# Attention and a three-way maxout layer: two steps' TensorE work issued together, the softmax normalised on ACT, output stages begun beside such a group

## The chip, the cores and the metric

The kernel runs on one core of one Trainium2 chip. The metric is the device time of one execution in microseconds. TensorE (PE, its weight loads PEld) multiplies matrices and transposes into PSUM, VectorE (DVE) and ScalarE (ACT) read PSUM and SBUF, GpSimd (POOL) works on SBUF only, and SyncE (SP) issues DMAs. POOL issues DMAs of its own too. Each engine works through its own queue in order, and semaphores hold an instruction until what it needs is there.

## The reference

There are two parts: a causal attention with a window of 128 positions and a distance bias per head, and on its output a layer that takes the maximum of three products and multiplies once more. Batch 8, 8 heads, 576 positions, 64 per head; 512 model columns, 768 hidden ones; all float32.

```python
scores = scale * np.matmul(q, k.transpose(0, 1, 3, 2))
bias = slopes[:, None, None] * (-np.abs(rel).astype(np.float32))[None, :, :]
mask = (rel >= 0) & (rel < window)
scores = np.where(mask, scores + bias[None], -1000000000.0)
scores = scores - np.max(scores, axis=-1, keepdims=True)
attn = np.exp(scores)
attn = attn / (np.sum(attn, axis=-1, keepdims=True) + 1e-09)
attn_out = np.matmul(attn, v)
# x: attn_out with the heads side by side, (8 * 576, 512)
h = np.maximum(np.maximum(x @ w1, x @ w2), x @ w3)
out = h @ w_out
```

## The kernel before, in words

**Attention.** A task t is one batch b and one pair of heads hp (32 tasks, four for each batch). A step (t, i) is a block of 128 query rows of a task, five for each task (the last has 64 rows), 160 steps in all. As the window is 128, a block of queries meets its own block of keys and the one before it. One step passes through four functions:

- `products` (L245) multiplies queries by keys on TensorE, 64 x 64 tiles side by side in the array, into the two banks of `scores`; one call covers two steps.
- `score` (L263): VectorE merges the two key blocks by a mask (L271 or L274), adds the bias and reduces to the row's extreme for each head (L286); ACT takes the exponential with a running sum into the tile p (L290, four buffers). After blocks 1, 3 and 4 it also adds 1e-9 to the sums (L296), takes the reciprocal (L299) and multiplies each p of the pair by it (L302), on POOL for even tasks of the first two batches and on VectorE otherwise.
- `turn` (L306): TensorE transposes p for both heads into the PSUM tile pt (L311, pool ps_t, one buffer); ACT copies it out (L315 for block 0, straight into pp; L318 into pr for the others); POOL cuts it into the two triangles of pp (L319, L323; four buffers).
- `mix` (L328) multiplies by v on TensorE (L345) into ps_x. After block 4 ACT copies the task's result to xk (L354).

**Dense layers.** Both products are done blockwise with seven block products in place of eight. A unit u is one such block product (L496): six matmuls of 288 columns for the expert stage (63 units for each batch), nine for the output stage (14 for each batch). ACT copies some units' results out of PSUM (L505), `put` (L436) combines the others on VectorE (L443 to L460), and `factors_h` (L404) splits the hidden blocks into a rounded part on ACT (L371) and a rest on POOL (L372), called hs, that the output stage multiplies. `factors_x` (L377) does the same for a batch's attention output, called xs. The units use the three PSUM banks ps_m. In batch 0 the weights are also unpacked and split (`convert`, `sums`, `part`; 120 calls through `weights`), and written to DRAM; later batches stream them back by a DMA that POOL issues once a buffer of a ring of two is free (`stream`, L218).

**Order.** There is no scheduler at run time: the list `events` (from L511) holds (due, call) pairs, the calls are made in order of due time, and each engine's queue is the order of those calls. Time is counted in steps, each batch's attention shifted by SHIFT = (0, 2, 5). Step s makes products at s if s is even, score at s, turn at s + 4.3, mix of blocks 0 and 1 of a task 7.4 steps after block 1, of blocks 2 to 4 7.4 steps after block 4. Batch b's expert units begin at `ready[b]`, just behind its last mix, and are spread evenly up to `ready[b + 1]`; batch b's 14 output units begin there, O_PACE = 0.36 steps apart, with `factors_x` of the next batch ahead of them. So while units of batch b run, the attention of batch b + 1 runs between them. `weights` is called once a step at s + 0.2, and twice a unit in batch 0. PSUM's eight banks are all in use: three ps_m, two scores, one pt, two ps_x.

Of the kernel before, what the change touches and what calls it, by code (L numbers as in the profile page):

```python
# [8 lines left out]
F32 = mybir.dt.float32  # L9
# [3 lines left out]
AF = mybir.ActivationFunctionType  # L13
ALU = mybir.AluOpType
# [1 line left out]

NEG = 1.0e30
LOAD_I = 1
LAG_T, LAG_X = 4, 7
GROUPS = (1, 4)  # L20
SHIFT = (0, 2, 5)
O_PACE = 0.36
RING = 2


# [4 lines left out]
def attention_maxout_kernel(  # L30
# [11 lines left out]
    nc = tc.nc  # L42
    P = 128
    B, NP, _, _, S = qk.shape
# [5 lines left out]
    NB = (S + P - 1) // P  # L50
    rows = [min(P, S - i * P) for i in range(NB)]
# [17 lines left out]
    ps_t = ctx.enter_context(tc.tile_pool(name="ps_t", bufs=1, space=PSUM))  # L69
# [16 lines left out]
        out=prev, in_=prev, pattern=[[1, P]], compare_op=ALU.is_gt, fill=0.0,  # L86
# [150 lines left out]
    pn, pp, xp, xk, stats = {}, {}, {}, {}, {}  # L237
# [25 lines left out]
    def score(t, i):  # L263
        b, hp = tasks[t]
        n = rows[i]
        ps, a = banks.pop((t, i))
        if i:
            mask = prev[:n].bitcast(mybir.dt.uint8)
            if a is None:
                for x in ps:  # L270
                    nc.vector.copy_predicated(x[:n, P:2 * P], mask, x[:n, :P])  # L271
            else:
                both = scores[:n, :, a * 2 * P:(a + 1) * 2 * P]
                nc.vector.copy_predicated(  # L274
                    both[:, :, P:], mask.unsqueeze(1).broadcast_to([n, 2, P]), both[:, :, :P],
                )
        p = s_p.tile([P, 2, P], F32, name="p", bufs=4)

        if i % 2 == 0:
            stats[t] = st_p.tile([P, 3, 2, 2], F32, name="st"), []  # L280
        st, two = stats[t]
        a = len(two)
        two.append(p)
        for j in range(2):
            s = s_p.tile([P, P], F32, name="s", bufs=3)
            nc.vector.tensor_tensor_reduce(  # L286
                out=s[:n], in0=ps[j][:n, P:2 * P], in1=(bias if i else bias0)[:n, 2 * hp + j, :],
                scale=-0.125, scalar=3.0e38, op0=ALU.add, op1=ALU.min, accum_out=st[:n, 0, a, j:j + 1],
            )
            nc.scalar.activation(  # L290
                p[:n, j], s[:n], AF.Exp, bias=st[:n, 0, a, j:j + 1], scale=-1.0, accum_out=st[:n, 1, a, j:j + 1]
            )
        pn[t, i] = p
        if i % 2 == 0 and i + 1 < NB:
            return
        nc.vector.tensor_scalar(  # L296
            out=st[:n, 1, :a + 1], in0=st[:n, 1, :a + 1], scalar1=1e-9, scalar2=None, op0=ALU.add
        )
        nc.vector.reciprocal(st[:n, 2, :a + 1], st[:n, 1, :a + 1])  # L299
        e = nc.gpsimd if t < 2 * NP and t % 2 == 0 else nc.vector  # L300
        for a, p in enumerate(two):
            e.tensor_tensor(  # L302
                out=p[:n], in0=p[:n], in1=st[:n, 2, a].unsqueeze(2).broadcast_to([n, 2, P]), op=ALU.mult
            )

    def turn(t, i):  # L306
        n = rows[i]
        p = pn.pop((t, i))
        pt = ps_t.tile([P, 2, P], F32, name="pt")
        for j in range(2):  # L310
            nc.tensor.transpose(out=pt[:, j, :n], in_=p[:n, j], identity=ident[:n, :n])  # L311
        w = pp_p.tile([P, 2, 2, P], F32, name="pp")
        pp[t, i] = w
        if i == 0:
            nc.scalar.copy(out=w[:, :, 0, :n], in_=pt[:, :, :n])  # L315
            return
        r = s_p.tile([P, 2, P], F32, name="pr", bufs=2)
        nc.scalar.copy(out=r[:, :, :n], in_=pt[:, :, :n])  # L318
        nc.gpsimd.affine_select(  # L319
            out=pp[t, i - 1][:, :, 1, :n], in_=r[:, :, :n], pattern=[[0, 2], [-1, n]],  # L320
            compare_op=ALU.is_gt, fill=0.0, base=0, channel_multiplier=1,
        )
        nc.gpsimd.affine_select(  # L323
            out=w[:n, :, 0, :n], in_=r[:n, :, :n], pattern=[[0, 2], [1, n]],
            compare_op=ALU.is_ge, fill=0.0, base=0, channel_multiplier=-1,
        )
# [187 lines left out]
    def at(when, what, *args):  # L514
        events.append((when, len(events), what, args))

    n_steps = NP * NB
    shift = [SHIFT[min(b, 2)] for b in range(B)]
    for t, (b, hp) in enumerate(tasks):
        for i in range(NB):  # L520
            s = t * NB + i + shift[b]
            if i == LOAD_I and t + 2 < len(tasks):
                at(s - 0.4, load, t + 2)
            if i == NB - 1 and t + 1 < len(tasks):
                at(s - 0.4, load_v, t + 1)
            if i == 0 and 0 < t < NP:
                at(s - 1, slopes, t)
            if (t * NB + i) % 2 == 0:
                at(s, products, t * NB + i)
            at(s, score, t, i)  # L530
            at(s + LAG_T + 0.3, turn, t, i)
            last = next(e for e in GROUPS if e >= i)
            at(s + last - i + LAG_X + 0.4, mix, t, i)

    ready = [n_steps * (b + 1) - 1 + LAG_X + 0.5 + shift[b] for b in range(B)]
    when = ready[0]
    for b in range(B):
        if b == 0:
            at(when, factors_x, 0, 0, 0)

        pace = (ready[b + 1] - when) / 63 if b + 1 < B else O_PACE
        for u in range(77 * b, 77 * b + 77):
# [3 lines left out]
            at(when, unit, u)  # L546
            when += pace if u < 77 * b + 63 else O_PACE
    for u in range(77 * B, 77 * B + 3):
# [49 lines left out]
```

## Time and profile before

| what | us |
|---|---|
| median of three runs | 872.14 |
| the runs | 865.38, 872.14, 874.06 |
| the profiled execution | 869.13 |
| its span, first to last instruction | 867.4 |
| granted TensorE clock, mean | 0.951 |

The profiled execution's own time lies 1.7 us above its span. The page gives each engine's busy time over the span; a busy TensorE may still be a slow one, as matmuls overlap and the modelled ends of the records are counted. In the table of stretches each engine has its busy time and, in brackets, its number of instructions; behind them stand the granted clock, the share of the DMA engines and GB/s. A group row names line, engine, operation, tiles and shape, then count, busy time and mean ns, then the idle time of the engine just ahead and who ended it. A wait row gives the total, the number of waits and the longest one.

### The profile page before, as it was taken

The numbers are of one execution on the slowest core, as the hardware profiler recorded it, in microseconds if no ns is written. First come the engines' busy times: TensorE is split into PE (matmuls) and PEld (weight loads), VectorE is DVE, ScalarE is ACT, GpSimd is POOL, SyncE is SP. The second block draws the span as 40 slices with busy tenths as digits, with TensorE's granted clock in tenths as the row PEclk, the third lists the DMA queues.
The fourth block names the chain that finished last, engine by engine and source line by source line (L and its number), as shares of the span: only waits on it lengthen the run. The fifth ranks groups of instructions, "written<-read, shape, count | busy, mean of one in ns | idle before, by whom it ended". The sixth has DMA issues, their size and how long they took to land.

```text
span 867.4 us, 17966 instructions
## 1 busy us (share of the span) xinstructions
PE 789.2 (91%) x6272; PEld 680.3 (78%) x6272; DVE 622.1 (72%) x1954; ACT 460.6 (53%) x1502; POOL 356.2 (41%) x580
## 2 busy tenths in 40 slices
PE   4779786777999999999999999999999999999897
PEld 2347565656988888887988798987889788989887
DVE  5789998899767866778577956777567957483452
ACT  6768666756555544555445544555456545442232
POOL 3543353213155423544255514544255525541332
PEclk7978897967999999999999999999999999999999
DMA  6653675662578638883577737883678537765761
GB/s 215 219 192 127 229 253 214 229 245 76 188 263 273 232 113 270 279 284 115 194 258 269 249 107 256 268 292 117 221 258 293 187 125 245 247 235 168 257 203 56
DMA packets 43402, 184.80 MB, mean 213 GB/s; under 512 B 4784, under 2 KB 13744, under 8 KB 34096
## 3 DMA queue, kind: packets, MB, share of 16 engines
q0 software_dynamic: 18144, 115.61, 39.9%
q1 hardware_dynamic: 25024, 67.97, 21.8%
q8 instruction: 50, 0.82, 0.4%
q14 instruction: 40, 0.33, 0.1%
q10 hardware_dynamic: 144, 0.07, 0.0%
HBM read 157.68 MB, written 25.95 MB: 212 GB/s over the span
## 4 chain that ended last, share of the span: by engine, by line
PE 60%; DVE 10%; issue 6%; ACT 6%; POOL 5%; DMA 3%; POOLq 0%; ACTq 0%; DVEq 0%; SPq 0%
PE ps_m L496 47%; PE ps_x L345 6%; PE ps_s L256 4%; POOL hs L372 3%; PE pt L311 3%; ACT p L290 2%; DMA wt<-keep 2%; DVE p L302 2%; DVE hq L458 1%; POOL pp L319 1%; DVE t L457 1%; ACT hs L371 1%; DVE t L375 1%; POOL pp L323 1%; DMA hs<-in_w_all 1%
## 5 line engine op out<-in xcount | busy, mean ns | idle before, releaser
L496 PE MATMUL ps_m<-xs,wt 128*128 128x288 f32 x3024 | 461.6, 306 | 22.3 <-DVE t L457 7.6
L496 PEld LDWEIGHTS ps_m<-xs,wt 128*128 128x128 f32 x3024 | 419.0, 192 | 53.8 <-DVE t L457 11.6
L290 ACT ACTIVATE p<-s,st 128x128 f32<-128x128 f32 (+1 forms) x320 | 126.0, 396 | 102.1 <-PE pt L311 78.2
L505 ACT COPY t<-ps_m 128x288 f32<-128x288 f32 x264 | 103.9, 398 | 138.3 <-PE ps_m L496 137.7
L496 PE MATMUL ps_m<-hs,ow 128*128 128x288 f32 x1008 | 156.3, 307 | 12.7 <-POOL hs L372 7.3
L496 PEld LDWEIGHTS ps_m<-hs,ow 128*128 128x128 f32 x1008 | 139.9, 193 | 25.9 <-POOL hs L372 11.4
L218 POOL DMA_DIRECT2D wt<-keep x126 | 69.8, 554 | 214.6 <-PE ps_m L496 170.5
L372 POOL TENSOR_TENSOR hs<-hq,hs 128x288 fp32r<-128x288 f32 x120 | 105.8, 890 | 51.6 <-ACT hs L371 51.3
L319 POOL TENSOR_SCALAR_AFFINE_SELECT pp<-pr 128x256 f32<-128x256 f32 (+1 forms) x128 | 63.3, 495 | 131.8 <-ACT pr L318 121.4
L345 PE MATMUL ps_x<-pp,v 128*64 128x256 f32 (+3 forms) x768 | 89.0, 338 | 15.7 <-POOL pp L319 13.1
L457 DVE TENSOR_TENSOR t<-ps_m,t 128x288 f32<-128x288 f32 x144 | 64.9, 451 | 43.2 <-PE ps_m L496 41.2
L286 DVE CUSTOM_DVE_ANT_0 s<-ps_s,bias 128x128 f32<-128x128 f32 (+1 forms) x300 | 77.7, 281 | 17.9 <-ACT p L290 12.7
L323 POOL TENSOR_SCALAR_AFFINE_SELECT pp<-pr 128x256 f32<-128x256 f32 (+1 forms) x128 | 65.2, 509 | 50.8 <-PE ps_x L345 50.8
L345 PEld LDWEIGHTS ps_x<-pp,v 128*64 128x64 f32 (+1 forms) x768 | 47.6, 140 | 42.9 <-POOL pp L319 18.0
L371 ACT CAST hs<-hq 128x288 fp32r<-128x288 f32 x120 | 50.2, 430 | 57.2 <-DVE hq L375 36.0
L256 PE MATMUL ps_s<-qk 64*64 64x192 f32 (+1 forms) x1080 | 69.6, 338 | 8.8 <-DVE st L286 4.7
L311 PE MATMUL pt<-ident,p 128*128 128x128 f32 (+1 forms) x320 | 64.1, 283 | 14.6 <-POOL p L302 7.7
L302 DVE TENSOR_TENSOR p<-p,st 128x256 f32<-128x256 f32 (+1 forms) x140 | 71.9, 545 | 1.8
L458 DVE TENSOR_TENSOR hq<-t,hq 128x288 f32<-128x288 f32 x144 | 70.0, 486 | 2.3
L274 DVE COPY_PREDICATED ps_s<-prev,ps_s 128x256 f32<-128x256 uint8 x120 | 50.4, 420 | 27.2 <-PE ps_s L256 26.3
L311 PEld LDWEIGHTS pt<-ident,p 128*128 128x128 f32 (+1 forms) x320 | 40.3, 145 | 30.9 <-POOL p L302 13.6
L290 ACT ACTIVATION_READ_ACCUMULATOR p<-s,st 128x1 f32 (+1 forms) x320 | 60.4, 189 | 0.0
(54 smaller groups left out, 714.0 us busy)
## 6 DMA issues: line engine op xcount, KB each, us to landing
wt<-keep POOLq DMA_DIRECT2D x63, 1024.0 KB, 7.0
wt<-keep POOLq DMA_DIRECT2D x63, 768.0 KB, 4.7
qk<-in_qk SPq DMA_DIRECT2D x31, 576.0 KB, 5.3
hs<-in_w_all SPq DMA_DIRECT2D x24, 512.0 KB, 5.9
v<-in_v SPq DMA_DIRECT2D x32, 320.0 KB, 4.7
keep<-wt SPq DMA_DIRECT2D x9, 1024.0 KB, 3.9
outT<-t SPq DMA_DIRECT2D x64, 144.0 KB, 1.8
keep<-wt SPq DMA_DIRECT2D x9, 768.0 KB, 5.1
```

Of the source, the lines that this page charges most:

```text
L256: nc.tensor.matmul(ps[j][d:d + D, o:o + k1 - k0], lhsT=qkt[t][j * D:(j + 1) * D, 0, q0:q0 + D], rhs=qkt[t][j * D:(j + 1) * D, 1, k0:k1], s ...
L286: nc.vector.tensor_tensor_reduce(out=s[:n], in0=ps[j][:n, P:2 * P], in1=(bias if i else bias0)[:n, 2 * hp + j, :], scale=-0.125, scalar=3. ...
L290: nc.scalar.activation(p[:n, j], s[:n], AF.Exp, bias=st[:n, 0, a, j:j + 1], scale=-1.0, accum_out=st[:n, 1, a, j:j + 1])
L302: e.tensor_tensor(out=p[:n], in0=p[:n], in1=st[:n, 2, a].unsqueeze(2).broadcast_to([n, 2, P]), op=ALU.mult)
L311: nc.tensor.transpose(out=pt[:, j, :n], in_=p[:n, j], identity=ident[:n, :n])
L323: nc.gpsimd.affine_select(out=w[:n, :, 0, :n], in_=r[:n, :, :n], pattern=[[0, 2], [1, n]], compare_op=ALU.is_ge, fill=0.0, base=0, channel ...
L345: nc.tensor.matmul(x[j * D:(j + 1) * D, c:c + e - a], lhsT=vv[:n, i, j * D:(j + 1) * D], rhs=w[:n, j].rearrange("p a b -> p (a b)")[:, a:e ...
L372: e.tensor_tensor(out=lo, in0=src, in1=hi.bitcast(F32), op=ALU.subtract)
L457: nc.vector.tensor_tensor(out=s, in0=ps, in1=e, op=ALU.add)
L458: nc.vector.tensor_tensor(out=h, in0=s, in1=h, op=ALU.max)
L496: nc.tensor.matmul(ps, lhsT=lt, rhs=rt, start=i == 0 and k in (0, 1, 4), stop=i == len(pairs) - 1, skip_group_check=True,)
L505: nc.scalar.copy(out=e, in_=ps)
```

## The change

Three constants change, `score` is cut in three, `turn` uses one pt tile for two steps, and the due times are rewritten. A step s with c = s rounded down to even: turn is due at c + 4.02, products at c + 0.03, score at s + 0.04; the sums and reciprocals at s + 0.5, the normalising at s + 0.9. The mixes are due at an even step plus 6.01. So at each even step stand together, in this order: a mix (of two or three blocks, or none), two turns, the products of two steps, a score. The normalising is done by ACT, one operation for each head of each step, with the reciprocal as its scale. `ready` is an even step plus 0.05, so the output units of a batch and the expert units behind them begin next to such a group.

```diff
@@ -16,10 +16,10 @@
-LAG_T, LAG_X = 4, 7
+LAG_T, LAG_X = 4, 6
 GROUPS = (1, 4)
-SHIFT = (0, 2, 5)
-O_PACE = 0.36
+SHIFT = (0, 2, 4)
+O_PACE = 0.285
 RING = 2
@@ -291,22 +291,29 @@
         pn[t, i] = p
-        if i % 2 == 0 and i + 1 < NB:
-            return
+
+    def sums_of(t, i):
+        n = rows[i]
+        st, two = stats[t]
+        a = len(two) - 1
         nc.vector.tensor_scalar(
             out=st[:n, 1, :a + 1], in0=st[:n, 1, :a + 1], scalar1=1e-9, scalar2=None, op0=ALU.add
         )
         nc.vector.reciprocal(st[:n, 2, :a + 1], st[:n, 1, :a + 1])
-        e = nc.gpsimd if t < 2 * NP and t % 2 == 0 else nc.vector
+
+    def normalise(t, i):
+        n = rows[i]
+        st, two = stats[t]
         for a, p in enumerate(two):
-            e.tensor_tensor(
-                out=p[:n], in0=p[:n], in1=st[:n, 2, a].unsqueeze(2).broadcast_to([n, 2, P]), op=ALU.mult
-            )
+            for j in range(2):
+                nc.scalar.activation(p[:n, j], p[:n, j], AF.Copy, scale=st[:n, 2, a, j:j + 1])
 
     def turn(t, i):
         n = rows[i]
         p = pn.pop((t, i))
-        pt = ps_t.tile([P, 2, P], F32, name="pt")
+        if (t * NB + i) % 2 == 0:
+            pn["pt"] = ps_t.tile([P, 2, 2, P], F32, name="pt")
+        pt = pn["pt"][:, (t * NB + i) % 2]
         for j in range(2):
             nc.tensor.transpose(out=pt[:, j, :n], in_=p[:n, j], identity=ident[:n, :n])
@@ -525,14 +532,19 @@
-            if (t * NB + i) % 2 == 0:
-                at(s, products, t * NB + i)
-            at(s, score, t, i)
-            at(s + LAG_T + 0.3, turn, t, i)
-            last = next(e for e in GROUPS if e >= i)
-            at(s + last - i + LAG_X + 0.4, mix, t, i)
-
-    ready = [n_steps * (b + 1) - 1 + LAG_X + 0.5 + shift[b] for b in range(B)]
+            c = s - (t * NB + i) % 2
+
+            at(c + LAG_T + 0.02, turn, t, i)
+            if s == c:
+                at(c + 0.03, products, t * NB + i)
+            at(s + 0.04, score, t, i)
+            if i % 2 or i + 1 == NB:
+                at(s + 0.5, sums_of, t, i)
+                at(s + 0.9, normalise, t, i)
+            e = t * NB + next(min(e + 1, NB - 1) for e in GROUPS if e >= i)
+            at(e - e % 2 + shift[b] + LAG_X + 0.01, mix, t, i)
+
+    ready = [n_steps * (b + 1) - 2 + LAG_X + 0.05 + shift[b] for b in range(B)]
```

## The prediction

> **What bounds the kernel now.** I read the table of stretches first, because the work of the eight batches differs: batch 0 also prepares the weights, the last stretch has no attention left.
>
> ```profile
> span 867.4 us, 17966 instructions
> PE 789.2 (91%) x6272; PEld 680.3 (78%) x6272; DVE 622.1 (72%) x1954; ACT 460.6 (53%) x1502; POOL 356.2 (41%) x580
> ```
>
> ```profile
> core 0: us, PE busy (x) PEld busy (x) DVE busy (x) ACT busy (x) POOL busy (x), PEclk, DMA share, GB/s
> 0.00:62.00 62.00, 39.02 (x312) 20.11 (x312) 45.56 (x196) 42.12 (x150) 27.39 (x54) 0.83 0.62 219
> 62.00:220.00 158.00, 124.98 (x820) 98.72 (x820) 141.14 (x421) 105.05 (x309) 54.86 (x74) 0.82 0.52 189
> 220.00:319.00 99.00, 98.17 (x843) 86.68 (x843) 73.39 (x254) 53.53 (x190) 42.80 (x75) 1.00 0.67 228
> 319.00:414.40 95.40, 93.13 (x771) 81.71 (x771) 68.35 (x217) 48.52 (x167) 40.92 (x69) 0.98 0.66 224
> 414.40:509.80 95.40, 93.11 (x790) 82.28 (x788) 69.32 (x220) 49.71 (x171) 42.52 (x71) 1.00 0.66 225
> 509.80:605.20 95.40, 93.12 (x792) 82.30 (x786) 69.33 (x220) 49.71 (x171) 42.56 (x71) 1.00 0.67 225
> 605.20:700.50 95.30, 92.99 (x789) 82.17 (x786) 69.44 (x220) 49.62 (x171) 42.71 (x71) 1.00 0.68 226
> 700.50:767.00 66.50, 65.83 (x540) 59.72 (x535) 40.51 (x122) 30.46 (x98) 30.01 (x54) 1.00 0.71 232
> 767.00:867.00 100.00, 88.86 (x645) 86.57 (x640) 45.05 (x90) 31.84 (x79) 32.43 (x43) 0.98 0.51 175
> ```
>
> Three regimes are to be seen. Until 62 us no engine is full: chains set the time. From 62 to 220 us VectorE is busy 141.14 of 158 (89%) with the weights. From 220 to 767 us TensorE is everything: its idle time in the six rows is 547.0 - 536.35 = 10.7 us at a granted clock near 1.00, and the middle rows repeat every 95.4 us. From 767 us on no attention is left, and the change touches nothing there. So in the middle 547 us any new TensorE wait is paid in full, and what the change can win there by removing waits is 10.7 us.
>
> The waits of TensorE in that stretch, then the pieces of attention as the timeline shows them among the expert (xs) and output (hs) units:
>
> ```profile
> PE ps_m L496 <- POOL hs L372: 6.7, 5, 1.6
> PE ps_m L496 <- DVE hq L452: 2.0, 5, 0.4
> PE ps_m L496 <- ACT t L505: 1.7, 6, 0.4
> ```
>
> ```profile
> 502.94 0.78 PE L256 MATMUL ps_s<-qk 64*64 64x128 f32 x16
> 503.64 1.46 PE L496 MATMUL ps_m<-hs,ow 128*128 128x288 f32 x9
> 504.94 0.38 PE L311 MATMUL pt<-ident,p 128*128 128x128 f32 x2
> 505.08 3.82 PE L496 MATMUL ps_m<-hs,ow 128*128 128x288 f32 x27
> 508.74 0.38 PE L311 MATMUL pt<-ident,p 128*128 128x128 f32 x2
> 509.05 1.25 PE L345 MATMUL ps_x<-pp,v 128*64 128x256 f32 x16
> 510.23 1.85 PE L496 MATMUL ps_m<-xs,wt 128*128 128x288 f32 x12
> ```
>
> From start to start, a unit's matmul takes (508.74 - 505.08) / 27 = 0.136 us; a turn (two transposes) between units hardly delays them: the next unit starts 0.14 us after it. The nine matmuls behind the products take 504.94 - 503.64 = 1.30 us where 9 x 0.136 = 1.22 is normal: leaving a group of small tiles costs 0.08 us once more. That is the whole price that grouping can save on the array.
>
> **The change, part by part.**
>
> **1. Two turns in a row, through one bank: the main term.** turn(a) issues two transposes, ACT's copy out of pt and, for i>0, POOL's selects; then turn(b) does the same, with nothing between them, as both events have one due time. Both write halves of one pt tile, and that tile, 2 x 2 x 128 floats, is one bank. I take it that the transposes of turn(b) wait until ACT has read the half of turn(a). Before, the next turn came a step later, behind units. What such a wait costs when the turns do follow one another, the start-up shows:
>
> ```profile
> 51.20 0.35 ACT L318 COPY pr<-pt 128x256 f32<-128x256 f32 x1
> 51.60 0.44 PE L311 MATMUL pt<-ident,p 128*128 128x128 f32 x2 [0.59 <-ACT pr L318]
> 52.15 0.37 ACT L318 COPY pr<-pt 128x256 f32<-128x256 f32 x1 [0.60 <-PE pt L311]
> 52.65 0.20 PEld L311 LDWEIGHTS pt<-ident,p 128*128 128x128 f32 x2 [0.39 <-ACT pr L318]
> ```
>
> Transposes end 52.04, copy 0.11 later, next transposes 1.05 after the first. At the clock of the middle stretch the pair takes 0.38 (row at 508.74), so 0.38 + 0.11 + 0.36 for the copy + 0.05 to TensorE (51.55 to 51.60) = 0.90 us. Unhindered, the second pair would start about 0.22 us after the first (estimate: two transposes, 0.11 each). The wait is 0.68 us, and everything behind turn(b) on TensorE's queue, the products and the units, waits with it. In those start-up rows the two turns used the pool's one buffer after each other; two halves of one tile occur in no row, so this reading is the fork of the prediction (first rival).
>
> The Trainium skill bears on the fork: "PSUM — Partial Sum Buffer", section "PSUM bank collisions raise a hardware error", asks that accesses of two engines be kept apart by bank and quadrant, not by address. By it the wait stands; no run here shows halves yet.
>
> To the 0.68 us come, per group:
> - The order inside a group is mix, turn, turn, products. Where the mix ends a head pair (2 groups of 5: per ten steps there are four mixes, two of them final), ACT copies xk ahead of turn(a)'s copy: from 0.05 to 0.69 us after the mix's end, while turn(a) ends about 0.31 after it and its copy would start at 0.42. That is +0.27 us in 2 of 5, +0.10 on average.
>
> ```profile
> L354 ACT COPY xk<-ps_x 128x576 f32<-128x576 f32 x23 | 14.7, 637 | 0.3
> L290 ACT ACTIVATE p<-s,st 128x128 f32<-128x128 f32 (+1 forms) x224 | 88.2, 396 | 92.8 <-PE pt L311 78.2 <-DVE st L286 13.5 <-PE ps_x L345 0.3
> ```
>
> - The normalise events stand 0.1 step ahead of the group in 3 of 5 groups, so that two or four ACT operations can stand ahead of turn(a)'s copy. They have the shape of the exponentials (396 ns, with a bias and a sum besides), so 0.30 to 0.40 us each, up to 1.6 us; the last unit and the mix (1.18 us, from 509.05 to 510.23) run meanwhile. I take +0.10 on average; bounds 0 and 0.5.
> - Leaving a group of small tiles once less: -0.08.
>
> The sum is 0.80 us per group. L290's 224 activations in the middle stretch are 112 steps, so 56 groups: **+45 us**. Bounds per group: 0.50 (nothing of ACT in front, and the drained array delays turn(a) anyway by 0.1) to 1.1, or 28 to 62 us.
>
> **2. The waits that go.** With an attention group ahead of the output stage's first unit, the wait for POOL's hs (6.7 us) is covered. exp of step s now finds its p buffer free, because turn(s-4) is issued ahead of score(s), where ACT stood 78.2 us for it. VectorE, which loses 113 normalise operations here, comes earlier with hq. At most 10.7 us can be won, as TensorE is idle no longer; I take **-8 us** (0 to -11).
>
> **3. Normalising on ACT.** 160 steps with two ACT operations each are 320, at 0.30 to 0.40 us about 96 to 128 us on ACT over the span. In a 95.4 us row ACT goes from 49.7 to about 64 us: beside TensorE, at no cost but the one in part 1. VectorE and POOL lose theirs:
>
> ```profile
> L302 DVE TENSOR_TENSOR p<-p,st 128x256 f32<-128x256 f32 (+1 forms) x113 | 59.9, 562 | 1.8
> L302 DVE TENSOR_TENSOR p<-p,st 128x256 f32<-128x256 f32 (+1 forms) x17 | 7.7, 485 | 0.0
> L302 DVE TENSOR_TENSOR p<-p,st 128x256 f32<-128x256 f32 (+1 forms) x10 | 4.3, 457 | 0.0
> L302 POOL TENSOR_TENSOR p<-p,st 128x256 f32<-128x256 f32 (+1 forms) x12 | 10.4, 885 | 17.7 <-DVE st L299 16.1 <-ACT p L290 1.6
> L302 POOL TENSOR_TENSOR p<-p,st 128x256 f32<-128x256 f32 (+1 forms) x9 | 7.9, 893 | 13.2 <-DVE st L299 13.2
> ```
>
> (The groups of 220 to 767, 62 to 220 and 0 to 62 us; the last two are POOL's of 0 to 62 and 62 to 220.) The 59.9 us lie beside TensorE and buy nothing. Before 220 us VectorE is rid of 4.3 + 7.7 = 12 us, the best that can come of it. "ScalarE: Activation LUTs", in the Trainium skill (section "Rules for kernel authors"), puts multiplications on VectorE, which speaks against this part; no row here compares the two for this operation.
>
> **4. The start.** In 0 to 62 us ACT is busy 42.12 us; 22 normalise operations become 44 on ACT, +13 to +17 us, so 55 to 59 of 62: ACT becomes nearly full there. Also, where t is odd, turn follows its normalise by as little as 1.1 steps, before by 3.3 or more, so products queue behind a turn that waits for ACT, which waits for VectorE's reciprocal behind the weights: what follows on each other is then 0.8 (products, row at 502.94) + 1.1 (mask 0.42, two reductions with their read-outs) + 0.8 (two exponentials with theirs) + 0.4 (sum, reciprocal) + 1.4 (normalise) + 1.1 (turns).
>
> ```profile
> L274 DVE COPY_PREDICATED ps_s<-prev,ps_s 128x256 f32<-128x256 uint8 x120 | 50.4, 420 | 27.2 <-PE ps_s L256 26.3
> L286 DVE CUSTOM_DVE_ANT_0 s<-ps_s,bias 128x128 f32<-128x128 f32 (+1 forms) x300 | 77.7, 281 | 17.9 <-ACT p L290 12.7
> L290 ACT ACTIVATE p<-s,st x320: 384/397/417, 7.7 to 739.2; 128x128 f32<-128x128 f32 x128, 64x128 f32<-64x128 f32 x32
> L290 ACT ACTIVATE p<-s,st 128x128 f32<-128x128 f32 (+1 forms) x44 | 17.3, 395 | 4.1 <-DVE st L286 4.1
> ```
>
> That is 5.6 us per group of two steps in half the groups, against 4.9 now: the last row is of 0 to 62 us, 22 steps, the first at 7.7 us, so (62 - 7.7) / 11. For six groups that is +4, with weights' operations in between up to +10. From 62 to 220 us VectorE sets the pace and gains up to 7.7. Together I take **+3 us**, bounds -12 and +10.
>
> **5. LAG_X, SHIFT, O_PACE** reorder the same instructions, among them the loads on SP's queue and the weights' DMAs on POOL's: both are issued by unit or step as before. The 14 output units are spread over 4 steps, not 5. Where TensorE is full, this moves no time; DMA runs at 0.66 of its engines. Zero; the cover is that the weights are fetched a ring of two ahead; if it failed, a fetch's 4.7 to 7.0 us would stand open once a block.
>
> ```profile
> wt<-keep POOLq DMA_DIRECT2D x63, 1024.0 KB, 7.0
> wt<-keep POOLq DMA_DIRECT2D x63, 768.0 KB, 4.7
> ```
>
> The sum: 45 - 8 + 3 = +40 us on the profiled execution's own 869.13 us, so **909 us**. The three runs of before lie at 865.38, 872.14 and 874.06; the profiled one lies 3 us below their median, which I leave in the range. About 1% is what a measurement of this kernel tells from no change (860 to 878 us).
>
> **The rivals.**
> - **A, faster: the halves are tracked apart.** Then the four transposes follow at 0.11 us, no wait arises, and only savings are left: 0.08 x 45 groups with a mix = -4, the idle time -11, the start +3: **857 us** (845 with the start's best). For it: the halves are disjoint columns, and a dependence by address would let them pass. Against it: ACT would read a bank that TensorE is writing; and part 1's rows show TensorE waiting for just this copy. Chance 0.12.
> - **B, no difference: the wait is at its lower bound and all else goes well.** 28 - 11 - 12 = +5: **874 us**. For it: VectorE at 89% until 220 us, freed of 12 us. Against: ACT nearly full in the start. Chance 0.10.
> - **C, much slower: ACT gates every group.** ACT runs in order; if the normalise operations wait for the reciprocal until the mix is over, turn(a)'s copy stands behind up to 1.6 us in 3 of 5 groups: 1.1 x 56 = 62, no idle time won back (-3), start +10: **938 us**. For it: ACT waits for VectorE 13.5 us already. Against: sums are issued 0.4 step (2 us) ahead of the normalising. Chance 0.15.
>
> **How the numbers follow.** The forecast has 0.63, with a range of its own of 885 to 925. The range 860 to 934 leaves out the better part of A and C's upper half. Faster by over 1%: 0.10 (most of A); within 1%: 0.13 (B, the rest of A and the forecast's low end); slower: 0.77.
>
> **What would show each step.** Part 1: in the middle stretch, groups of two and two transposes 0.9 to 1.2 us apart, and TensorE (or its weight load) waiting for ACT pr or pp for some 35 to 45 us in total, where now it waits none; a repeating stretch of about 102 us in place of 95.4. Part 2: no wait for POOL hs at the outputs. Part 3: VectorE's 71.9 us of L302 gone, ACT at 560 to 590 us. Part 4: the first expert unit between 58 and 72 us. The prediction is wrong if the four transposes run 0.11 us apart, or if the stretch repeats in under 96 us.

## The result, and the profile after

The changed kernel takes 902.2 us, median of four runs (901.31 to 904.1), against 870.9 us before, also four runs; the ratio of the means is 1.0369, 95% interval 1.0311 to 1.0427. It is slower. The forecast was 909 us.

The page's head after the change, and the stretches. In the second fence the first two rows are the two parts of the start (up to the first expert unit, then up to the first expert matmul of batch 1), the third is the middle (up to that of batch 7), the fourth the tail, the fifth one repeating stretch; the fence behind it has the middle and one stretch of the kernel before, cut at the same places. The columns: the stretch and its length in us, then busy us and instructions of PE, PEld, DVE, ACT and POOL, the granted clock, the DMA share and GB/s.

```profile
span 899.6 us, 18013 instructions
PE 819.5 (91%) x6272; PEld 682.5 (76%) x6272; DVE 566.5 (63%) x1814; ACT 554.8 (62%) x1822; POOL 328.5 (37%) x560
```

```profile
0.00:67.60 67.60, 47.69 (x315) 23.16 (x315) 43.28 (x193) 54.21 (x198) 16.19 (x42) 0.84 0.59 201
67.60:218.30 150.70, 118.38 (x813) 94.54 (x813) 132.38 (x387) 114.74 (x343) 41.23 (x62) 0.86 0.56 202
218.30:821.20 602.90, 582.90 (x4634) 496.40 (x4634) 358.33 (x1165) 362.41 (x1222) 246.26 (x422) 1.00 0.63 209
821.20:899.60 78.40, 70.52 (x514) 68.34 (x513) 32.50 (x70) 23.43 (x60) 24.86 (x35) 1.00 0.55 186
...
422.40:524.40 102.00, 98.63 (x788) 83.41 (x785) 60.02 (x200) 62.00 (x211) 41.77 (x71) 1.00 0.63 211
```

```profile
222.20:785.70 563.50, 551.20 (x4608) 489.72 (x4608) 400.93 (x1262) 289.73 (x983) 249.24 (x418) 1.00 0.67 224
414.90:510.20 95.30, 93.01 (x788) 82.21 (x784) 69.30 (x221) 49.61 (x171) 42.49 (x72) 1.00 0.66 226
```

The two profiled executions differ by 901.31 - 869.13 = 32.2 us. The start gives 218.3 against 222.2 (-3.9), the middle 602.9 against 563.5 (+39.4), the tail 78.4 against 81.8 (-3.4). The same matmuls need 102.0 us where they needed 95.3; the granted clock is the same. TensorE's idle time grew only from 12.3 to 20.0 us, while its busy time grew by 31.7 us: most of the loss hides as busy. The timeline of TensorE shows how; each fence row is a run of matmuls of one kind, and the last two groups shown are those in which TensorE stands idle longest ahead of a transpose.

```profile
439.08 1.08 PE L352 MATMUL ps_x<-pp,v 128*64 128x256 f32 x8
440.10 0.44 PE L318 MATMUL pt<-ident,p 128*128 128x128 f32 x2
440.47 0.55 PE L256 MATMUL ps_s<-qk 64*64 64x192 f32 x6
441.06 0.34 PE L318 MATMUL pt<-ident,p 64*128 64x64 f32 x2
441.32 0.86 PE L256 MATMUL ps_s<-qk 64*64 64x192 f32 x10
442.11 6.66 PE L503 MATMUL ps_m<-xs,wt 128*128 128x288 f32 x48
...
480.24 0.44 PE L318 MATMUL pt<-ident,p 128*128 128x128 f32 x2
480.61 0.77 PE L256 MATMUL ps_s<-qk 64*64 64x128 f32 x14
482.23 0.44 PE L318 MATMUL pt<-ident,p 128*128 128x128 f32 x2 [0.85 <-ACT pr L325]
...
499.68 0.44 PE L318 MATMUL pt<-ident,p 128*128 128x128 f32 x2
500.05 0.76 PE L256 MATMUL ps_s<-qk 64*64 64x192 f32 x10
501.45 0.44 PE L318 MATMUL pt<-ident,p 128*128 128x128 f32 x2 [0.64 <-ACT pp L322]
```

The two turns of a group start 0.96 us apart (440.10 and 441.06), and up to 1.99 us (480.24 and 482.23); over the 58 groups of the middle the mean is 1.17 us. Between them stands a part of the products, which by its due time belongs behind both: so TensorE's queue is not simply the order of the calls, as I had taken it to be. The instructions were laid out anew when the program was built, it seems by when each was expected to be ready; the products are cut in two around a turn that would wait. The same happened to mixes. Of eight mixes in a stretch, one is in two pieces and one in three: TensorE changes to ps_x 11 times, not 8, and to ps_s 19 times, not 12. The waits ahead of its weight loads, then ahead of its matmuls, 220 to 800 us:

```profile
PEld pt L318 <- ACT pr L325: 20.2, 47, 1.2
PEld ps_m L503 <- DVE hq L467: 6.9, 5, 1.4
PEld pt L318 <- ACT pp L322: 6.7, 11, 1.0
PEld ps_m L503 <- POOL hs L379: 3.4, 4, 0.9
```

```profile
PE pt L318 <- ACT pr L325: 4.3, 6, 0.9
PE pt L318 <- ACT pp L322: 4.0, 6, 0.7
PE ps_m L503 <- DVE st L302: 3.5, 3, 1.2
PE ps_m L503 <- POOL hs L379: 2.4, 4, 0.6
PE ps_m L503 <- DVE hq L467: 2.2, 2, 1.2
PE ps_m L503 <- ACT t L512: 0.9, 1, 0.9
```

58 waits of the weight loads of transposes for ACT's copy, 26.9 us, are new. The units' matmuls wait 9.0 us in all, where the rows of before (in the prediction, 220 to 767 us) have 10.4: the wait for POOL's hs shrank from 6.7 to 2.4 us, and waits for VectorE (hq and st) grew in its place.

### The profile page after: what moved, and what is told of

Read it like the earlier page. It is cut to its first block, busy times and chain, and to the rows that moved or that the text cites. A ratio compares the mean times of both kernels' runs of the same rounds, so it can differ in the third digit from the quotient of the medians.

```text
span 899.6 us, 18013 instructions
## 1 busy us (share of the span) xinstructions
PE 819.5 (91%) x6272; PEld 682.5 (76%) x6272; DVE 566.5 (63%) x1814; ACT 554.8 (62%) x1822; POOL 328.5 (37%) x560
## 4 chain that ended last, share of the span: by engine, by line
PE 54%; DVE 10%; ACT 6%; POOL 6%; issue 5%; DMA 4%; POOLq 0%; ACTq 0%; DVEq 0%
PE ps_m L503 41%; PE ps_s L256 5%; POOL hs L379 5%; PE ps_x L352 5%; PE pt L318 3%; DMA wt<-keep 2%; DMA hs<-in_w_all 2%; ACT hs L378 2%; DVE st L299 2%; DVE t L382 1%; DVE t L464 1%; DVE hq L465 1%; ACT p L290 1%; ACT p L309 1%; ACT t L512 1%
## 5 line engine op out<-in xcount | busy, mean ns | idle before, releaser
L503 PE MATMUL ps_m<-xs,wt 128*128 128x288 f32 x3024 | 444.4, 302 | 28.1 <-ACT t L512 8.5
L503 PEld LDWEIGHTS ps_m<-xs,wt 128*128 128x128 f32 x3024 | 413.1, 190 | 58.3 <-issue 16.5
L503 PE MATMUL ps_m<-hs,ow 128*128 128x288 f32 x1008 | 147.3, 302 | 16.0 <-DVE t L464 6.6
L326 POOL TENSOR_SCALAR_AFFINE_SELECT pp<-pr 128x256 f32<-128x256 f32 (+1 forms) x128 | 55.7, 436 | 233.1 <-ACT pr L325 229.6
L309 ACT ACTIVATE p<-p,st 128x128 f32<-128x128 f32 (+1 forms) x320 | 108.2, 395 | 18.6 <-DVE st L302 18.0
L256 PE MATMUL ps_s<-qk 64*64 64x192 f32 (+1 forms) x1080 | 93.6, 348 | 8.0 <-DMA qk<-in_qk 4.3
L325 ACT COPY pr<-pt 128x256 f32<-128x256 f32 (+1 forms) x128 | 44.1, 345 | 89.0 <-PE pt L318 85.5
L352 PE MATMUL ps_x<-pp,v 128*64 128x256 f32 (+3 forms) x768 | 94.6, 342 | 2.4 <-POOL pp L326 1.8
L318 PE MATMUL pt<-ident,p 128*128 128x128 f32 (+1 forms) x320 | 70.7, 300 | 20.2 <-ACT pr L325 8.2
L352 PEld LDWEIGHTS ps_x<-pp,v 128*64 128x64 f32 (+1 forms) x768 | 47.7, 141 | 31.7 <-issue 12.7
L256 PEld LDWEIGHTS ps_s<-qk 64*64 64x64 f32 x1080 | 45.9, 139 | 32.3 <-issue 20.7
```

Of the source, the lines that this page charges most:

```text
L256: nc.tensor.matmul(ps[j][d:d + D, o:o + k1 - k0], lhsT=qkt[t][j * D:(j + 1) * D, 0, q0:q0 + D], rhs=qkt[t][j * D:(j + 1) * D, 1, k0:k1], s ...
L309: nc.scalar.activation(p[:n, j], p[:n, j], AF.Copy, scale=st[:n, 2, a, j:j + 1])
L352: nc.tensor.matmul(x[j * D:(j + 1) * D, c:c + e - a], lhsT=vv[:n, i, j * D:(j + 1) * D], rhs=w[:n, j].rearrange("p a b -> p (a b)")[:, a:e ...
L503: nc.tensor.matmul(ps, lhsT=lt, rhs=rt, start=i == 0 and k in (0, 1, 4), stop=i == len(pairs) - 1, skip_group_check=True,)
```

## The experiments

Theory W: the second turn of a group waits for ACT's copy out of the same bank, and the loss is this wait with what the build made of it. Its rivals: grouping and due times themselves (G), the normalising on ACT (N). For each run the table has the start, the repeating stretch (a third of the time from the first expert matmul of batch 3 to that of batch 6) and the tail of its profiled execution, and the medians with their ratios to the kernel before on the same chip. The start is less sure than the stretch: it is that of one execution, in which the granted clock changes many times (a mean of 0.80 in run 2, 0.86 in run 11), and executions of one kernel differ by up to 12 us (run 11: 853.6 to 865.54). A few us between two starts therefore do not show what an edit does.

| kernel | start | stretch | tail | median | ratio (95%) |
|---|---|---|---|---|---|
| before | 222.2 | 95.34 | 81.8 | 870.9 | |
| changed | 218.3 | 102.01 | 78.4 | 902.2 | 1.0369 (1.0311 to 1.0427) |
| 1 transposes first | 216.4 | 96.75 | 79.4 | 872.06 | 1.0015 (0.9992 to 1.0038) |
| 2 normalising back | 223.9 | 100.83 | 78.9 | 898.5 | 1.0323 (1.0271 to 1.0375) |
| 3 second turn behind products | 217.6 | 96.60 | 79.4 | 872.83 | 1.0025 (1.0003 to 1.0047) |
| 4 before, products cut | 227.6 | 96.74 | 78.2 | 879.21 | 1.0102 (1.0064 to 1.0140) |
| 5 before, normalising on ACT | 228.1 | 94.07 | 78.6 | 863.53 | 0.9901 (0.9876 to 0.9925) |
| 6 = 1, mix behind products | 213.0 | 94.40 | 79.2 | 859.19 | 0.9873 (0.9810 to 0.9937) |
| 7 = 1, mix half a step later | 218.9 | 93.86 | 79.2 | 861.61 | 0.9886 (0.9835 to 0.9936) |
| 8 = 6, ACT for nine tasks only | 215.8 | 95.39 | 79.1 | 866.84 | 0.9949 (0.9921 to 0.9976) |
| 9 changed, mix half a step later | 218.0 | 102.68 | 81.5 | 901.43 | 1.0312 (1.0239 to 1.0385) |
| 10 before, ACT from task nine | 223.6 | 94.18 | 78.7 | 859.86 | 0.9845 (0.9783 to 0.9906) |
| 11 = 7, with 6's mixes in two batches | 218.6 | 93.86 | 78.4 | 858.53 | 0.9832 (0.9754 to 0.9909) |

**1. Transposes of both steps first, then both copies.**

```diff
+        pn[t, i] = pt
+
+    def turned(t, i):
+        n = rows[i]
+        pt = pn.pop((t, i))
         w = pp_p.tile([P, 2, 2, P], F32, name="pp")
@@
             at(c + LAG_T + 0.02, turn, t, i)
+            at(c + LAG_T + 0.025, turned, t, i)
```

> The changed kernel with each turn cut in two events: the transposes of both steps first, then both copies and selects. So no transposes wait for ACT's copy of the same bank. Theory W (the slowdown is this wait, and what the build made of it: the products of a group cut in two around the second turn, with two more switches between whole and small tiles): the repeating stretch of 101.9 us falls to 93 to 96 us, the time to 860 to 872 us. Rival G (the grouping and the new due times cost by themselves) or N (normalising on ACT costs): it stays above 890 us.

The time came to 872.06 us, the stretch to 96.75 us: the loss is gone but for 0.15%, so W holds against G and N. Time and stretch lie a little above the top of what I expected: the stretch is still 1.4 us longer than before, and the whole middle 10.7 us (574.2 against 563.5), which a shorter start and tail hide in this execution. That part was not foreseen. The timeline shows four transposes of 0.66 us together and whole products, but a mix in three pieces.

```profile
463.31 0.86 PE L357 MATMUL ps_x<-pp,v 128*64 128x256 f32 x6
464.11 1.86 PE L508 MATMUL ps_m<-xs,wt 128*128 128x288 f32 x12
465.90 0.60 PE L357 MATMUL ps_x<-pp,v 128*64 128x64 f32 x8
466.43 0.66 PE L318 MATMUL pt<-ident,p 128*128 128x128 f32 x4
467.01 0.78 PE L256 MATMUL ps_s<-qk 64*64 64x128 f32 x16
```

**2. The changed kernel with the normalising back on VectorE and POOL** (the diff's four lines of `normalise` undone, due times kept).

> The changed kernel with the normalising back on VectorE and POOL, as before, at its new due times. Theory W: the groups keep their shape, the time stays within 895 to 906 us. Rival N (ACT's 320 more operations delay the copies that TensorE waits for): below 885 us.

898.5 us: N is not the cause. In the stretch ACT's normalising costs 1.2 us here (102.01 against 100.83). The start is 5.6 us shorter with it, but run 2's profiled execution took 3.3 us more than its median, so this size is not sure.

**3. The second turn behind the products.**

```diff
-            at(c + LAG_T + 0.02, turn, t, i)
+            at(c + LAG_T + (0.02 if s == c else 0.035), turn, t, i)
```

> The changed kernel with the second turn of a group due behind the products instead of ahead of them. The bank and the wait's cause stay, but 0.8 us of products cover it and the products stay whole. Theory W: 862 to 874 us, within 1% of the run with the transposes first. If the wait alone counted and not the cut of the products, the same; if the grouping or ACT's load were the cause, above 890 us.

872.83 us. The bank is shared as before, and covering the wait with whole products is worth as much time as removing it, though the cover is not complete: from 220 to 770 us this row stands at 18.9 us in 44 waits in the changed kernel, and here at

```profile
PEld pt L318 <- ACT pr L325: 14.2, 35, 1.2
```

So the sum of these waits is not the loss: three quarters of this row are left, and all of the loss but 0.25% is gone. Such a wait seems to cost little while TensorE still works through products.

**4. Before, with products in two halves and a turn between them.**

```diff
-                at(s, products, t * NB + i)
-            at(s, score, t, i)
-            at(s + LAG_T + 0.3, turn, t, i)
+                at(s, products, t * NB + i, 0)
+                at(s + 0.02, products, t * NB + i, 1)
+            at(s + 0.03, score, t, i)
+            at(s + LAG_T + (0.3 if (t * NB + i) % 2 else 0.01), turn, t, i)
```

> The kernel before with only this: the products of two steps are issued in two halves, and the turn of the even step, whose bank has been free for a step, stands between the halves. No wait is added, two switches of tile shape are. If the cut costs 0.2 to 0.3 us in each of the 56 groups of the middle, 880 to 888 us; if in the changed kernel only the wait for ACT's copy costs, no change (866 to 874 us).

(`products` makes one step's half of them at each call.) 879.21 us, 1.0% slower: a cut costs something without any such wait, 1.4 us in a stretch of ten cuts, or 0.14 us each, where I had expected 0.2 to 0.3. So of the 5.3 us that run 1 took away in a stretch, the nine cuts of products would be about a quarter. The rest falls to the wait by subtraction; no run has the wait without anything else.

**5. Before, with only the normalising moved to ACT**, where it stood in `score`.

> The kernel before with only the normalising moved to ACT, issued where it stood, at the end of the score of blocks 1, 3 and 4. The start (up to the first expert unit of batch 1) takes 222.2 us before, 223.9 with the groups and the normalising on VectorE and POOL, 216.4 to 218.3 with the groups and ACT. If ACT's part is the cause of that gain it shows here too: start 215 to 219 us. In the middle ACT has room (about 64 of 95 us): stretch of 95.3 to 96.5 us. Together 863 to 873 us. If ACT's queue in the way of the units' copies costs more than that, above 880 us.

863.53 us, 1% faster, as expected in total, but by other parts than expected. The start did not shrink but grew by 5.9 us, so nothing here says that the changed kernel's shorter start is ACT's work alone. The stretch shrank by 1.3 us. Its middle:

```profile
228.10:783.40 555.30, 550.94 (x4609) 490.04 (x4608) 353.02 (x1149) 352.65 (x1209) 239.45 (x418) 1.00 0.68 228
```

TensorE's busy time is that of before (551.2 us), its idle time fell from 12.3 to 4.4 us: with VectorE 48 us less busy, the waits for hs and for VectorE shrink. (Some 1.5 us of the 8.2 by which the middle shrank are the clock's: before, it was granted at half for some 3 us from 399 us on.)

**6, 7. Run 1 with each mix due behind the products, or half a step later.**

```diff
-            at(e - e % 2 + shift[b] + LAG_X + 0.01, mix, t, i)
+            at(e - e % 2 + shift[b] + LAG_X + 0.045, mix, t, i)
```

(For the second, 0.5, with `ready` half a step later and five pp buffers.)

> The run with the transposes first, and besides each mix due behind the products instead of ahead of the turns. In that run the build cut three of eight mixes in two in each stretch (11 visits to ps_x, not 8), since their last block's selects come late; behind the products the order has no cut. Theory W with this as the second loss: each cut costs about 0.8 us, so the stretch falls from 96.75 to 93 to 94.5 us and the time to 850 to 862 us. If the cuts cost nothing and the long runs of units are what takes back the gain, it stays at 868 to 874 us.

> The run with the transposes first, the mix due half a step later, alone between units (the pool pp with five buffers, ready half a step later). The mixes are whole again, but leave the group. By the cuts alone the stretch falls to 94 to 95 us, 855 to 865 us; if a mix inside the group saves a switch of tiles, this is slower than the run with the mix behind the products by 0.1 us in 45 groups, 4 to 5 us.

859.19 and 861.61 us, both faster than before by a little over 1%. Mixes are whole in both, and the stretch is 2.4 and 2.9 us shorter than in run 1. But whole mixes are not all of it, as the units' waits ahead of TensorE's matmuls, 320 to 700 us (four stretches), show. Run 1:

```profile
PE ps_m L508 <- DVE hq L472: 5.6, 4, 1.4
PE ps_m L508 <- ACT t L517: 3.0, 4, 0.8
PE ps_m L508 <- POOL hs L384: 2.8, 4, 0.7
```

Run 6, mix behind products:

```profile
PE ps_m L508 <- DVE hq L472: 5.8, 4, 1.5
PE ps_m L508 <- DVE hq L464: 2.3, 4, 0.6
```

They sum to 11.4 us in run 1, 8.1 in run 6 and 4.8 in run 7: 0.8 us less in a stretch of run 6, 1.65 in one of run 7. That leaves at most 1.2 to 1.6 us in a stretch for the cuts of mixes; the rest is units that wait less in the new order. That a mix inside the group saves a switch isn't to be seen; the run without that has the shorter stretch.

**8. Run 6 with ACT normalising in the first nine tasks only.**

> The run with the mix behind the products, and the normalising on ACT only for the first nine tasks (up to some 220 us), on VectorE after. Normalising on ACT seems to cost 1.0 us in a stretch of the changed kernel (102.0 against 100.8 with VectorE). If that is ACT's queue ahead of the copy that TensorE waits for, it is gone here already and nothing changes (within 0.4%); if ACT's load itself slows the units, 4 to 6 us less than the run with the mix behind the products.

866.84 us: neither came, it is 7.6 us slower than run 6. With no transposes waiting for ACT's copies, normalising on ACT gains 1.0 us in a stretch. This run says something else too: with whole groups and VectorE normalising in the middle, as before, the stretch is 95.39 us, and it was 95.34: grouping by itself gains nothing.

**9. The changed kernel with only the mixes half a step later** (as in run 7, with `ready` and five pp buffers), the wait kept.

> The changed kernel, its turns as they are (copy of the first turn between the transposes), with each mix due half a step later so that the build leaves it whole. If the loss of the changed kernel is a sum of the mixes' cuts (96.75 to 93.86 us in a stretch without the wait, 2.9 us) and of the wait with the cut products (5.2 us), the stretch falls from 102.0 to 99.1 us and the time to 882 to 888 us. If the late turn and the cut mix are one loss counted twice, it falls to 95 to 97 us, below 872 us.

901.43 us and a stretch of 102.68: a miss. Mixes are whole, and nothing is won. Two things take it back. First, one group in each stretch: its turns stand 2.97 us apart, where the changed kernel's longest is 1.99, because the first turn's copy begins 2.2 us after its transposes, behind other work of ACT. In the other nine the distance is the same or smaller. The same row in the changed kernel and in this one, 320 to 700 us:

```profile
PEld pt L318 <- ACT pr L325: 13.9, 30, 1.2
```

```profile
PEld pt L318 <- ACT pr L325: 18.3, 30, 2.3
```

That is 1.1 us of the missing 3.6 in a stretch. Second, the clock. Right behind that group the granted clock falls to half for some 3 us, from 477, 579 and 682 us on, once in each of the three periods (from batch to batch) that the stretch averages; in the changed kernel it stays at 1.00. The same 8 us of the changed kernel and of this one, clock third from the end:

```profile
476.00:484.00 8.00, 7.15 (x62) 5.40 (x62) 5.73 (x13) 5.39 (x19) 5.58 (x9) 1.00 0.66 217
476.00:484.00 8.00, 8.00 (x54) 6.94 (x53) 3.44 (x15) 4.16 (x15) 3.28 (x7) 0.79 0.55 207
```

In the kernel before, the one period of the middle with such a spell (at 399 us) takes 96.9 us and the next 95.3, so a spell costs about 1.5 us; run 9's two periods without one take 100.2 and 101.1 us. What sets the spells off, and the remaining 1 us, stay open. Without the spells, the losses of the wait and of the mixes would miss adding up by about 2 us in a stretch.

**10, 11. Two faster kernels put together.** Before with ACT's normalising from the tenth task on (`if t < 9` keeps the old lines, on POOL for every even task), and run 7 with run 6's mixes in the first two batches.

> The kernel before, with the normalising on ACT from the tenth task on only, on POOL and VectorE by turns before it. On ACT throughout, the start grew from 222.2 to 228.1 us and the stretch shrank from 95.34 to 94.07 us. If the two are separate, the start is back at 221 to 223 us and the stretch stays near 94.1: 855 to 860 us. If the start's loss lies elsewhere: 861 to 866 us.

> The run with the transposes first, mixes behind the products in the first two batches (start of 213.0 us there) and half a step later after (stretch of 93.86 us there). If start and stretch add up: 850 to 856 us, the fastest so far. If the start's 213.0 us hang on what follows, 857 to 863 us.

859.86 us with a stretch of 94.18, near what was expected: the gain lies in the middle, and by these two executions the loss in the start is gone (223.6 against 228.1). 858.53 us for the other: the stretch came (93.86), the start of 213.0 us did not (218.6). Whether that start hangs on what follows is not shown: run 6's profiled execution is its fastest, 2.7 us under its median, and run 11 has five pp buffers in place of four. These and run 6 lie within each other's intervals, at 1.3 to 1.7% under the kernel before; three lines moved to ACT are enough for it.

## Why the prediction was right, step by step

**Step 1, the wait between the two turns: the mechanism was right, its cost too large, and the build's part was missed.** The transposes do wait for ACT's copy out of the other half of their bank. The Trainium skill's "PSUM — Partial Sum Buffer" (section "PSUM bank collisions raise a hardware error") asks for a guard by bank and quadrant, not by address; the rows above, with 58 such waits and none in run 1, agree. The distance between the turns was nearly right as well: 0.90 us and 0.20 for ACT's other work make 1.10, and 1.17 was measured. What failed is that all of it was counted as lost, 0.80 us per group. Run 1 takes away 5.26 us per ten groups, 0.53 each: the build filled part of the wait with products, at the price of cutting them. Over the middle (602.9 to 574.2) that is 29 us where I had 45. What made good for it was something I had nothing for: the order of mixes and units. Run 7 takes 2.9 us more out of a stretch, 14.5 out of the middle (574.2 to 559.7), of which the cuts of mixes are at most about half.

So the middle's +39.4 us is 28.7 + 14.5 and -3.8, by which run 7 lies under the kernel before. That this comes near the forecast's 45 - 8 = 37 is in part luck: a term too large by 16 us and one left out nearly cancel. The split also holds only in the order in which the parts were removed.

**Step 2, -8 us for waits that go: nearly all of it did not come.** In the changed kernel the units' waits ahead of TensorE's matmuls fell only from 10.4 to 9.0 us: the one for hs fell as argued, but hq and st took its place. The 8 us can be had: in run 5, TensorE's idle time in the middle falls by 7.9 us, with the turns where they were. There it is the normalising leaving VectorE that frees these waits, not the group ahead of the output stage nor the earlier p buffer.

**Step 3, "the 59.9 us lie beside TensorE and buy nothing": wrong.** They buy 1.3 us in a stretch by run 5, 1.0 by runs 6 and 8. In the changed kernel the same move costs 1.2 us (run 2); there TensorE waits for ACT, and from 220 to 770 us the transposes' waits for pr are 18.9 us, the longest 1.2, where run 2 has 16.3 and 0.5. The rule of "ScalarE: Activation LUTs" (the Trainium skill, section "Rules for kernel authors") that multiplications belong on VectorE does not hold for this kernel's middle.

**Step 4, the start: +3 us forecast, -3.9 measured,** within its bounds. Normalising on ACT alone goes with a longer start (run 5, +5.9), as I argued; with the groups it goes with a shorter one (changed against run 2, -5.6). Both are differences between two executions, and no run takes the start apart, so this step stays open.

**Step 5 and the tail.** The tail's -3.4 us I do not count for the change: run 9, with the changed kernel's turns, has 81.5 us, run 5, with the order of before, 78.6.

**The rivals.** A's reading (no wait between halves) is refuted, but its number, 857 us, is nearly what the kernels without the wait reach once mixes are whole. (The 845 beside it is mis-added; the start's best would give 842.) C, ACT ahead of the copy, is true of a few groups: in three of ten the copy begins 0.9 to 1.1 us after the transposes. In one of these, normalising that waits for the reciprocal stands ahead of it, as the last section shows; in the other two it is xk and casts of hs.

**The signs named in advance** came for the most part: turns 0.9 to 1.1 us apart in half of the groups (two in ten at 0.74, three in ten at 1.75 to 2.0), a stretch of 102 us, the first expert unit at 67.6 us, the normalising's VectorE time gone. The wait for hs did not vanish. ACT came to 554.8 us, just under the 560 to 590 given, and the new waits to 26.9 us, not 35 to 45.

## What to carry to other kernels

Putting two users of one PSUM bank next to each other on TensorE made a round trip through the reader out of each pair here (0.53 us lost per pair); issue all writes of a bank first, or put the next independent work between them, whole. When instructions are laid out by a model at build time, read the order that came of it before crediting a grouping, because a wait can show up as cut groups and as busy time. And price a move between engines in the order in which it will run: the same normalising on ACT gained 1.3 us in a stretch where no transpose waited for ACT's copy, and lost 1.2 us where some did.

## What the hardware showed beyond that

The longest wait in the changed kernel, at 480.24, begins with a VectorE instruction on 64 x 2 numbers. The timeline rows of POOL, VectorE and ACT ahead of it:

```profile
478.06 2.32 POOL L379 TENSOR_TENSOR hs<-hq,hs 128x288 fp32r<-128x288 f32 x3
```

```profile
477.93 2.47 DVE L299 TENSOR_SCALAR st<-st 64x2 f32<-64x2 f32 x1 [0.74 <-ACT p L290]
480.44 0.16 DVE L302 RECIPROCAL st<-st 64x2 f32<-64x2 f32 x1
```

```profile
480.69 0.69 ACT L309 ACTIVATE p<-p,st 64x128 f32<-64x128 f32 x2 [1.84 <-DVE st L302]
481.29 0.62 ACT L361 COPY xk<-ps_x 128x576 f32<-128x576 f32 x1
481.81 0.36 ACT L325 COPY pr<-pt 128x256 f32<-128x256 f32 x1
```

```profile
L299 DVE TENSOR_SCALAR st<-st x96: 151/165/2754, 12.8 to 783.9; 128x4 f32<-128x4 f32 x64, 64x2 f32<-64x2 f32 x32
```

The addition has a median of 165 ns and takes 2.47 us here; it ends with the third of three POOL operations in a row (478.06 + 2.32 = 480.38). So it was in each of the last five batches that run attention, at 2.47 to 2.75 us. It was so in runs 1, 2 and 3 too (2.47 to 3.05 us). The reciprocal is late, then ACT's normalising, then xk, then the first turn's copy, and the second turn stands 0.85 us idle. The Trainium skill, "Advanced Engine Details and Errata", section "VectorE Performance Modes", says that VectorE's second SBUF port is shared with GpSimd, and that GpSimd's instructions and VectorE's two-port ones block each other; the rows fit, but they don't show in which mode this addition ran, and no run tried it apart.
